# An attention and gated-MLP kernel: values and scores joined, and new slots for attention and operands

## The chip, the cores and the metric

One core of a Trainium2 chip runs the whole program in one launch. The metric is the device time of that core in microseconds. Three runs of the kernel before are given, and one further execution was profiled; all rows come from that execution.

## The reference

Eight batches of eight heads with 576 positions of 64 numbers go through attention in chunks of 64 positions, and the result, 4608 tokens of 512 numbers, through a two-layer MLP with a gate. All is in fp32.

```python
scores = scale * np.matmul(q_c, k_c.transpose(0, 1, 2, 4, 3))   # 64 x 64 per chunk
scores = scores - np.max(scores, axis=-1, keepdims=True)
attn = np.exp(scores)
attn = attn / (np.sum(attn, axis=-1, keepdims=True) + 1e-09)
out = np.matmul(attn, v_c)
...
h = x @ w_in                        # 4608 x 512 by 512 x 2048
g = h * np.clip(h + 3.0, 0.0, 6.0) / 6.0
return g @ w_out                    # 2048 x 512
```

## The kernel before

The tokens are split into nine blocks of 512. An attention (class `Attention`, line 122) handles one block n and one half dp of the heads: `scores` (line 144) makes 64 products of 64x64 into the two banks of one PSUM tile, `soft` (line 161) takes maximum, subtraction, exponential, sum and division in steps 0 to 4, `transpose` (line 187) turns the weights with eight products and a ScalarE copy, and `values` (line 204) makes 64 products of 64x64, which ScalarE copies out. Scores, turned weights and values all use the pool `ps_a`, which holds one such tile. For the blocks n < 3 VectorE then also subtracts the rounded copy from the PSUM tile, to get the low part of the operand (line 234). There are 18 attentions.

A large product is done in three passes of 128x512 fp32r products, high by high, high by low and low by high (`passes`, line 244), so every operand needs a rounded copy (ScalarE) and a remainder (VectorE). 

The work has three parts.

1. **Start** (lines 301 to 381): the two attentions of block 0 in an order written out by hand, with products on dummy data between (`warm_up`), and the first weights turned from 64-bit words into fp32 high and low parts (`convert`, line 99: two ScalarE instructions, shift and addition on VectorE, a ScalarE cast, a VectorE subtraction). Block 0's first product for the first of 16 hidden blocks is written out with it (`part`).
2. **Plain part** (lines 529 to 581): blocks 0 to 2. For each hidden block `ft` there are two slots: an even one with the first product (`mm1`, 12 products into one of the two banks of `ps_h`) and its gate (ReLU on ScalarE, minimum and product on VectorE), and an odd one with the second product of an earlier hidden block (`mm2`, 12 products into four banks of `ps_o`). Other work is put into these slots by number through `plan` (line 476): in each slot the steps of rank under 10 come ahead of the gate (`early_steps`), the others behind it (`late_steps`). During block 0 the weights of `ft + 2` are converted in the slot of `ft`; during blocks 1 and 2 `prepare` (line 401) makes weight combinations and stores them in HBM for the last part.
3. **Steady part** (lines 721 to 746): three superblocks of two blocks, each with a seven-product (Strassen-like) scheme. A superblock has 56 slots of the first product and 56 of the second, each slot six products. In the first product the products come in the order 1, 5, 6, 7, 2, 3, 4 for each of eight hidden pairs p; numbers 2, 3 and 4 go on adding into the banks of 1, 5 and 7, whose sums VectorE must have read by then (`add`, line 597). Number 6 uses `ps_h`, as does number 3 in the second product. Other work hangs at slots through `at` (line 589) and is issued behind the slot's products by rank (`tick`, line 717). `units` (line 654) makes the second product's 28 operand units (ScalarE copy and VectorE subtraction, `split`, line 444), `x_operands` (line 454) the seven operands of the next superblock, and two blocks of attention for the next superblock run meanwhile. GpSimd makes the differences of gated values.

Everything is issued in program order on each engine (`manual_schedule`), and a tile's buffer is taken over when its old readers are done. SyncE issues all transfers in one queue. In the plain part the old attention steps are put by this table and this rank, in which `args` is a list:

```python
later = [(-3, "load_qk"), (2, "scores"), (3, "tiles"), (3, "soft", 0), (3, "soft", 1), (3, "soft", 2), ...
put(at + s, ..., k if name in ("soft", "tiles", "load_qk", "load_v") and args != (2,) else 10 + k)
```

The old steady slots of the four attentions start at 6, 23, 40 and 78 of a superblock, with scores at 0, maximum 1, subtraction 2, sum 8, division 9, turning 12 and values 15 behind; unit k stands at slot 51 + int(1.75 k).

## Time and profile before

| | us |
|---|---|
| median of three runs | 809.33 |
| lowest and highest | 809.21, 809.99 |
| profiled execution | 809.08 |
| its span, first to last instruction | 807.2 |
| PE (TensorE) busy | 796.4 |
| DVE (VectorE) busy | 601.9 |
| ACT (ScalarE) busy | 366.9 |
| POOL (GpSimd) busy | 65.0 |

A busy TensorE is not TensorE at its peak: products overlap, and the end of one is modelled. The pace is read from the starts in the timeline. In a timeline row the columns are start, length, engine, line, operation, output and input tiles, shape and count, and in brackets the idle time of that engine just before, with what ended it. Equal neighbours are merged into one row with a count.

### The profile page before, as it was taken

The page shows a single profiled execution, that of the slowest core. Times are in us where ns is not written, and L with a number is a line of the kernel's source. Part 1 is how long each engine was busy: PE and PEld are TensorE (multiplying, and loading weights), DVE is VectorE, ACT ScalarE, POOL GpSimd, SP SyncE. Part 2 cuts the span into 40 slices and gives each one's busy share as a digit, 9 for nine tenths or more (in the row PEclk, how much of TensorE's full clock was granted, in tenths as well). Part 3 has the DMA queues.
Part 4 walks back from the last instruction along what each step waited for, and adds up shares of the span by engine and source line. Part 5 has one row for each costly group of instructions (what it writes and reads, how often), then busy time and mean ns, then how long its engine had stood idle before and what let it go on. Part 6 is the DMA issues. An engine that isn't in the chain of part 4 may idle for free.

```text
span 807.2 us, 13704 instructions
## 1 busy us (share of the span) xinstructions
PE 796.4 (99%) x5684; PEld 650.0 (81%) x5684; DVE 601.9 (75%) x771; ACT 366.9 (45%) x464; POOL 65.0 (8%) x55
## 2 busy tenths in 40 slices
PE   8999999999999999999999999999999999999997
PEld 5777888888888888888788888888788888888886
DVE  6889867897788682867888776778897856668941
ACT  5878644442453353344473433444634423347330
POOL 0000000000000000222110001222100012221000
PEclk9999999999999999999999999999999999999999
DMA  9980102968888753566556577665566665555463
GB/s 356 410 355 27 53 2 79 310 217 264 291 273 269 246 179 123 203 250 234 179 201 240 207 224 285 252 234 181 201 239 229 214 207 194 205 201 199 176 241 115
DMA packets 50157, 172.85 MB, mean 214 GB/s; under 512 B 4656, under 2 KB 16944, under 8 KB 39472
## 3 DMA queue, kind: packets, MB, share of 16 engines
q1 hardware_dynamic: 50096, 171.99, 60.3%
q8 instruction: 45, 0.74, 0.4%
q14 instruction: 16, 0.13, 0.0%
HBM read 133.17 MB, written 38.80 MB: 213 GB/s over the span
## 4 chain that ended last, share of the span: by engine, by line
PE 86%; DVE 7%; ACT 4%; DMA 1%; issue 1%; SPq 0%; DVEq 0%; ACTq 0%
PE acc L246 19%; PE acc L248 18%; PE acc L247 18%; PE h L246 8%; PE h L248 8%; PE h L247 8%; PE two L216 2%; PE two L154 2%; PE two L198 2%; DMA w<-w_in_out 1%; DVE u L109 1%; DVE u L597 1%; DVE g L609 1%; ACT r L106 1%; ACT u L105 1%
## 5 line engine op out<-in xcount | busy, mean ns | idle before, releaser
L246 PE MATMUL acc<-xop,ws 128*128 128x512 f32 x528 | 208.7, 395 | 0.5
L248 PE MATMUL acc<-xop,ws 128*128 128x512 f32 x528 | 205.7, 390 | 0.0
L247 PE MATMUL acc<-xop,ws 128*128 128x512 f32 x528 | 205.7, 390 | 0.0
L246 PEld LDWEIGHTS acc<-xop,ws 128*128 128x128 f32 x528 | 99.1, 188 | 24.2 <-DVE h L597 2.1
L248 PEld LDWEIGHTS acc<-xop,ws 128*128 128x128 f32 x528 | 99.1, 188 | 20.7
L247 PEld LDWEIGHTS acc<-xop,ws 128*128 128x128 f32 x528 | 99.2, 188 | 19.7
L447 DVE TENSOR_TENSOR xop<-g,xop 128x1024 fp32r<-128x1024 f32 x72 | 87.7, 1238 | 22.5 <-ACT xop L446 22.4
L446 ACT CAST xop<-g 128x1024 fp32r<-128x1024 f32 x72 | 73.2, 1051 | 38.7 <-PE acc L248 21.6
L617 POOL TENSOR_TENSOR g<-g 128x512 f32<-128x512 f32 x24 | 31.0, 1291 | 665.9 <-DVE g L609 665.9
L608 ACT ACTIVATE r<-acc,half 128x512 f32<-128x512 f32 x72 | 49.4, 686 | 71.9 <-DVE acc L597 71.9
L246 PE MATMUL acc<-g,w 128*128 128x512 f32 x192 | 76.3, 397 | 0.0
L246 PE MATMUL h<-x,w 128*128 128x512 f32 x188 | 74.2, 395 | 0.7 <-ACT w L114 0.7
L248 PE MATMUL acc<-g,w 128*128 128x512 f32 x192 | 74.9, 390 | 0.0
L247 PE MATMUL acc<-g,w 128*128 128x512 f32 x192 | 74.8, 390 | 0.0
L248 PE MATMUL h<-x,w 128*128 128x512 f32 x188 | 73.6, 391 | 1.2 <-DVE w L116 1.2
L247 PE MATMUL h<-x,w 128*128 128x512 f32 x188 | 73.2, 390 | 0.0
L609 DVE SCALAR_TENSOR_TENSOR g<-r,acc 128x512 f32<-128x512 f32 x72 | 49.0, 681 | 31.0 <-ACT r L608 31.0
L263 DVE SCALAR_TENSOR_TENSOR r<-r,h 128x512 f32<-128x512 f32 x48 | 32.7, 681 | 32.5 <-ACT r L262 32.5
L246 PE MATMUL h<-xop,ws 128*128 128x512 f32 x144 | 56.2, 391 | 0.0
L247 PE MATMUL h<-xop,ws 128*128 128x512 f32 x144 | 56.0, 389 | 0.0
L248 PE MATMUL h<-xop,ws 128*128 128x512 f32 x144 | 56.0, 389 | 0.0
L262 ACT ACTIVATE r<-h,half 128x512 f32<-128x512 f32 x48 | 32.8, 683 | 47.0 <-PE h L248 47.0
(86 smaller groups left out, 1163.9 us busy)
## 6 DMA issues: line engine op xcount, KB each, us to landing
ws<-b SPq DMA_DIRECT2D x42, 1024.0 KB, 4.8
ws<-a SPq DMA_DIRECT2D x24, 1024.0 KB, 4.9
ws<-a SPq DMA_DIRECT2D x24, 768.0 KB, 4.2
w<-w_in_out SPq DMA_DIRECT2D x16, 1024.0 KB, 18.0
qk<-qk_in SPq DMA_DIRECT2D x16, 1024.0 KB, 6.9
v<-v_in SPq DMA_DIRECT2D x17, 512.0 KB, 5.3
out_t<-o SPq DMA_DIRECT2D x32, 256.0 KB, 3.8
a<-hl SPq DMA_DIRECT2D x32, 256.0 KB, 3.0
```

What stands on the lines that cost most here:

```text
L154: PE.matmul(t[o, a, c if k is None else c % 4, :], lhsT=self.qk[rows, c // 4, 0, c % 4, o], rhs=self.qk[rows, c // 4, 1, c % 4, o], start= ...
L198: PE.transpose(out=self.tp[:, a, i], in_=self.e[:, a, 2 * i:2 * i + 2].rearrange("p c t -> p (c t)"), identity=ident)
L246: PE.matmul(ps, lhsT=a_h, rhs=b_h, start=first, stop=False, skip_group_check=more)
L247: PE.matmul(ps, lhsT=a_h, rhs=b_l, start=False, stop=False, skip_group_check=more)
L248: PE.matmul(ps, lhsT=a_l, rhs=b_h, start=False, stop=last, skip_group_check=more)
L262: ACT.activation(out=r, in_=h, func=AF.Relu, bias=half, scale=1.0 / 6.0)
L263: DVE.scalar_tensor_tensor(out=r, in0=r, scalar=1.0, in1=h, op0=ALU.min, op1=ALU.mult)
L446: ACT.copy(out=t[:, :, 0], in_=src)
L447: DVE.tensor_tensor(out=t[:, :, 1], in0=src, in1=t[:, :, 0].bitcast(F32), op=ALU.subtract)
L608: return (lambda: ACT.activation(out=r, in_=ps, func=AF.Relu, bias=half, scale=1.0 / 6.0), lambda: DVE.scalar_tensor_tensor(out=out, in0=r ...
L609: lambda: DVE.scalar_tensor_tensor(out=out, in0=r, scalar=1.0, in1=ps, op0=ALU.min, op1=ALU.mult))
L617: sub = lambda o, x, y: lambda: POOL.tensor_tensor(out=o, in0=x, in1=y, op=ALU.subtract)
```

## The change

- In the plain part the table PLAIN gives each of eight attentions its own slots (loads, scores, maximum, subtraction, exponential, sum, division, turning, values), and in the steady part STEADY does so for the four attentions of a superblock. Where the values of one attention and the scores of the next have the same slot, `visit` issues the 64 products of the values and the 64 of the scores one behind the other. The values then go to the two banks of `ps_h` (`own_banks`), and each bank is copied out by itself.
- The exponential has rank 10 in the plain part.
- In the steady part a slot may be a fraction: the whole part is the slot, the rest the rank. The unit and operand slots are written out (UNITS, MORE).
- The conversion of weights is a class with a method for each instruction. At the start its instructions for the first three weights, the loads, the first product's passes and the scores of the next block are put in another order; the conversion of the third weight begins at the start.

```diff
+PLAIN = ((0, 0, 0, 9, 10, 10, 12, 13, 16, 18),
+         (4, 14, 20, 21, 21, 22, 24, 24, 29, 30),
+         (31, 34, 36, 37, 37, 37, 38, 38, 42, 43),
+         (36, 44, 43, 45, 46, 47, 48, 48, 53, 55),
+         (52, 56, 55, 56, 56, 57, 58, 59, 64, 65),
+         (60, 65, 65, 66, 66, 66, 67, 67, 69, 71),
+         (67, 73, 71, 72, 72, 72, 73, 74, 78, 79),
+         (71, 80, 79, 80, 80, 80, 81, 81, 85, 86))
+STEADY = ((2.1, 6.6, 7.1, 7.5, 9.0, 12.0, 13.0, 19.1, 20.1),
+          (9.6, 23.3, 20.1, 22.5, 22.5, 30.0, 35.2, 40.6, 41.6),
+          (35.5, 52.0, 41.6, 41.9, 44.5, 47.9, 49.9, 54.6, 71.8),
+          (64.1, 78.6, 71.8, 75.6, 75.7, 78.9, 79.5, 83.6, 87.6))
+UNITS = (-2.9, -1.9, -1.8, 1.8, 3.0, 3.9, 6.4, 11.0, 11.5, 12.0, 12.2, 13.5, 14.1, 14.6, 14.9, 20.9, 23.9, 26.6, 27.5, 28.2, 29.5, 30.7, 32.1, 33.0, 34.6, 34.9, 35.2, 40.1)
+MORE = (43.9, 46.1, 48.2, 53.6, 54.3, 54.6, 56.7)
...
         def multiply(self, heads):
             if heads[0] == 0:
-                self.po = self.psum("o").rearrange("p s (a i t) -> p s a i t", a=2, t=CH)
+                t = self.psum("o")
+                self.apart = isinstance(t, list)
+                self.po = [b.rearrange("p (a i t) -> p a i t", a=2, t=CH) for b in (t if self.apart else [t[:, s] for s in range(2)])]
...
             if self.n >= NSTD:
                 if self.n not in xraw:
                     xraw[self.n] = raw.tile([P, NDP, 2, NT], F32, name="x")
-                ACT.copy(out=as_src(xraw[self.n][:, self.dp]), in_=src)
+                for src, to in parts:
+                    ACT.copy(out=to(xraw[self.n][:, self.dp]), in_=src)
                 return
...
-            ACT.copy(out=as_src(x[:, 0]), in_=src)
-            low.append(lambda: DVE.tensor_tensor(out=as_src(x[:, 1]), in0=src, in1=as_src(x[:, 0]).bitcast(F32), op=ALU.subtract))
+            for src, to in parts:
+                ACT.copy(out=to(x[:, 0]), in_=src)
+                low.append(lambda src=src, to=to: DVE.tensor_tensor(out=to(x[:, 1]), in0=src, in1=to(x[:, 0]).bitcast(F32), op=ALU.subtract))
...
+        load_w(0)
         b0.load_v()
-        load_w(0)
         load_w(1)
         b1.load_v(gp.tile([P, 2, NB // 2, 2 * CH], F32, name="g"))
+        load_w(2)
         a1[0].load_qk()
-        load_w(2)
         load_w(3)
...
+        c0.high()
+        c0.words()
+        b1.soft(0)
+        b1.soft(1)
+        c0.shift()
+        c0.add()
         warm_up(IDLE[3])
+        b1.soft(2)
         b0.turned([0])
         b0.turned([1])
...
+        c0.low()
         finish()
-        next(c1)
+        b1.turned([0])
+        b1.turned([1])
+        c1.shift()
+        c1.add()
+        c2.high()
+        c2.shift()
...
+        for k in (0, 2):
+            part(0, k)
+            part(1, k)
         b1.multiply([0])
         b1.multiply([1])
-        a1[0].scores()
...
+        c1.cast()
         finish()
+        c1.low()
+        c2.words()
+        part(0, 1)
+        part(1, 1)
+        for k in (0, 2, 1):
+            part(2, k)
+            part(3, k)
+            if k == 2:
+                a1[0].scores()
...
+    def own_banks(step):
+
+        return [ps_h.tile([P, NT], F32, name="h") for _ in range(2)] if step == "o" else two_banks(ps_a)
+
+    def visit(a, b):
+
+        a.multiply(range(2))
+        b.scores()
+        a.multiplied(range(2))
+
+    chain = a1 + [Attention(*which) for which in ((2, 0), (2, 1), (3, 0), (4, 0), (4, 1), (3, 1))]
+    for k, (a, slots) in enumerate(zip(chain, PLAIN)):
+        load_qk, load_v, scores, high, sub, exp, total, mult, turn, values = slots
...
+        for step, at in enumerate((high, sub, exp, total, mult)):
+            put(at, lambda step=step, a=a: a.soft(step), 10 if step == 2 else 3 + step)
+        put(turn, a.transpose, 15)
+        if k + 1 < len(PLAIN) and PLAIN[k + 1][2] == values:
+            a.psum = own_banks
+            put(values, lambda a=a, b=chain[k + 1]: visit(a, b), 16)
+        else:
+            put(values, a.values, 16)
...
     def at(slot, *f, rank=0):
 
-        todo.setdefault(slot, []).extend((rank, g) for g in f)
+        todo.setdefault(int(slot // 1), []).extend((slot % 1 + rank, g) for g in f)
...
-        for k in range(4 * 7):
-            at(base + SLOTS - 5 + int(1.75 * k), lambda k=k, unit=unit: unit(k), rank=1)
+        for k, t in enumerate(UNITS):
+            at(base + SLOTS + t, lambda k=k, unit=unit: unit(k))
...
-            for k in range(7):
-                at(base + SLOTS + 44 + 2 * k, more, rank=1)
+            for t in MORE:
+                at(base + SLOTS + t, more)
```

In the steady part `put_steady` puts the four attentions by STEADY in the same way, and a gate that stood in its slot behind nothing (`at(slot + 2, gate)`) now has rank 0.1. In the plain loop the conversion of `ft + 2` issues the same six instructions in the same places, except for `ft = 0`, where only addition, cast and low part are left.

## Rows read from the trace of the kernel before

**Rows 1.** The page: busy us, share of the span and instructions of TensorE.
```profile
PE 796.4 (99%) x5684; PEld 650.0 (81%) x5684; DVE 601.9 (75%) x771; ACT 366.9 (45%) x464; POOL 65.0 (8%) x55
```

**Rows 2.** Timeline of TensorE around one attention's values, late in the plain part.
```profile
283.27 0.39 PE L247 MATMUL h<-x,w 128*128 128x512 f32 x1
283.50 0.39 PE L248 MATMUL h<-x,w 128*128 128x512 f32 x1
283.82 1.16 PE L216 MATMUL two<-e,v 64*64 64x64 f32 x64
284.91 0.50 PE L246 MATMUL acc<-g,w 128*128 128x512 f32 x1
285.25 0.39 PE L247 MATMUL acc<-g,w 128*128 128x512 f32 x1
```

**Rows 3.** Timeline of TensorE at the start: values, then scores.
```profile
21.52 1.16 PE L216 MATMUL two<-g 64*64 64x64 f32 x64
22.50 1.11 PE L154 MATMUL two<-qk 64*64 64x64 f32 x64
```

**Rows 4.** The values' line: products x count, ns min/median/max, first and last start.
```profile
L216 PE MATMUL two<-e,v x1088: 217/218/268, 15.4 to 625.1; 64*64 64x64 f32 x182
```

**Rows 5.** Timeline of ScalarE behind the values of rows 2.
```profile
285.05 1.02 ACT L228 COPY x<-two 128x1024 f32<-128x1024 f32 x1 [0.37 <-PE two L216]
```

**Rows 6.** Groups by shape: half-size copy and half-size subtraction out of PSUM.
```profile
L233 ACT CAST x<-two 128x512 fp32r<-128x512 f32 x4 | 2.1, 585 | 1.0 <-PE two L216 1.0
...
L234 DVE TENSOR_TENSOR x<-two,x 128x512 fp32r<-128x512 f32 x4 | 2.6, 680 | 0.0
```

**Rows 7.** DMA issues on the page: transfers, KB each, median us to landing.
```profile
qk<-qk_in SPq DMA_DIRECT2D x16, 1024.0 KB, 6.9
```

**Rows 8.** Timeline of ScalarE in the plain part.
```profile
56.42 0.67 ACT L262 ACTIVATE r<-h,half 128x512 f32<-128x512 f32 x1
56.99 1.03 ACT L114 CAST w<-u 128x1024 fp32r<-128x1024 f32 x1
```

**Rows 9.** Timeline of TensorE in the plain part.
```profile
59.34 0.50 PE L248 MATMUL h<-x,w 128*128 128x512 f32 x1 [0.53 <-DVE w L116]
```

**Rows 10.** Timeline of VectorE at the start.
```profile
16.79 1.22 DVE L178 TENSOR_REDUCE z<-g 128x16 f32<-128x1024 f32 x1 [0.18 <-ACT g L176]
...
29.54 1.23 DVE L116 TENSOR_TENSOR w<-u,w 128x1024 fp32r<-128x1024 f32 x1 [0.51 <-ACT w L114]
```

**Rows 11.** Timeline of TensorE in the first products of two superblocks.
```profile
395.57 1.03 PE L198 MATMUL two<-ident,e 128*128 128x128 f32 x8
...
397.59 0.39 PE L248 MATMUL acc<-xop,ws 128*128 128x512 f32 x1
398.11 0.50 PE L246 MATMUL acc<-xop,ws 128*128 128x512 f32 x1
...
399.37 0.39 PE L248 MATMUL acc<-xop,ws 128*128 128x512 f32 x1
399.85 0.50 PE L246 MATMUL acc<-xop,ws 128*128 128x512 f32 x1
...
724.99 0.50 PE L246 MATMUL acc<-xop,ws 128*128 128x512 f32 x1
```

**Rows 12.** Timeline of VectorE in the same stretch of the first superblock.
```profile
392.55 1.94 DVE L185 TENSOR_TENSOR e<-e,z 128x1024 f32<-128x1024 f32 x1
...
395.01 1.72 DVE L447 TENSOR_TENSOR xop<-g,xop 128x1024 fp32r<-128x1024 f32 x1
396.65 0.68 DVE L597 TENSOR_TENSOR u<-h,p 128x512 f32<-128x512 f32 x1
397.36 0.69 DVE L597 TENSOR_TENSOR u<-acc,u 128x512 f32<-128x512 f32 x1
...
399.10 0.69 DVE L597 TENSOR_TENSOR h<-acc,u 128x512 f32<-128x512 f32 x1
```

**Rows 13.** Timeline of GpSimd there.
```profile
393.49 2.16 POOL L617 TENSOR_TENSOR t<-g 128x512 f32<-128x512 f32 x1
```

More of the change, by code (lines that the diff above doesn't have):

```diff
@@ L328, in tile_kernel @@
         b0.soft(3, 1)
-        next(c0)
         for a in range(2):
@@ L535, in tile_kernel @@
         over = []
-        c = convert(ft + 2, DVE) if ft + 2 < NFT else None
-        if c:
-            next(c)
-            next(c)
+        c = None
+        if ft + 2 < NFT:
+            c = Convert(ft + 2) if ft else c2
+            if ft:
+                c.high()
+                c.words()
+                c.shift()
+            c.add()
         gt = gate(h)
@@ L545, in tile_kernel @@
         if c:
-            next(c)
-            next(c)
+            c.cast()
+            c.low()
         if len(pending) >= LAG:
@@ L597, in add, with put_steady @@
         return lambda: DVE.tensor_tensor(out=out, in0=x, in1=y, op=ALU.add)
-    def put_steady(n, dp, at_):
-        a = Attention(n, dp)
-        for k, f in ((-6, a.load_qk), (0, a.load_v), (0, a.scores), (1, a.tiles), (1, lambda: a.soft(0)), (2, lambda: a.soft(1)), (2, lambda: a.soft(2)), (8, lambda: a.soft(3)),
-                     (9, lambda: a.soft(4)), (12, a.transpose), (15, a.values)):
-            at(at_ + k, f, rank=2)
+    def put_steady(first, base):
+        four = [Attention(first + k // 2, k % 2, steady_psum) for k in range(2 * NDP)]
+        for k, (a, slots) in enumerate(zip(four, STEADY)):
+            soft = lambda i, a=a: lambda: a.soft(i)
+            load_qk, load_v, scores, high, sub, total, mult, turn, values = (base + t for t in slots)
+            at(load_qk, a.load_qk)
+            at(load_v, a.load_v)
+            if not k or slots[2] != STEADY[k - 1][-1]:
+                at(scores, a.scores)
+            at(high, a.tiles, soft(0))
+            at(sub, soft(1), soft(2))
+            at(total, soft(3))
+            at(mult, soft(4))
+            at(turn, a.transpose)
+            if k + 1 < len(four) and STEADY[k + 1][2] == slots[-1]:
+                a.psum = own_banks
+                at(values, lambda a=a, b=four[k + 1]: visit(a, b))
+            else:
+                at(values, a.values)
     def gated(out, ps):
@@ L641, in first_product @@
                     at(slot + 1, add(acc[6], ps, u4), relu)
-                    at(slot + 2, gate)
+                    at(slot + 2, gate, rank=.1)
                 elif i == 2:
@@ L648, in first_product @@
                     at(slot + 1, add(ps, ps, u2), relu)
-                    at(slot + 2, gate)
+                    at(slot + 2, gate, rank=.1)
                     if i == 3:
-                        at(slot + 2, sub(out, out, gq(0, 0)), sub(t2[p // 2][:, p % 2], gq(1, 1), out))
+                        at(slot + 2, sub(out, out, gq(0, 0)), sub(t2[p // 2][:, p % 2], gq(1, 1), out), rank=.1)
                 tick(slot)
@@ L723, in tile_kernel @@
         if s + 1 < NSUP:
-            for k in range(2 * NDP):
-                put_steady(NSTD + 2 * s + 2 + k // 2, k % 2, base + (6, 23, 40, 78)[k])
+            put_steady(NSTD + 2 * s + 2, base)
         box = {}
```

105 lines of the change are left out of this document (47 added, 58 removed).

## The prediction

> **What bounds the kernel now.** I read the page's busy times first: TensorE works for 99% of the span [rows 1], so the other engines cost something only where TensorE waits for them, and the forecast is a count of what TensorE loses between its 128x512 products. For that I went through TensorE's timeline. A stream of such products starts one every 0.227 us: 283.27 to 283.50 [rows 2]. The same rows show what a small stretch costs. Sixty-four 64x64 products (the values of one attention) stand between the products that start at 283.50 and 284.91, 1.41 us apart, and the product behind them comes another 0.34 later. Beyond the stream's own two steps that is 1.18 + 0.11 = 1.29 us. Every lone values or scores stretch of the plain and steady parts repeats this within 0.06 us; there are 31 of them. The reader should see that the small products themselves don't fill the 1.29: the first of them starts 0.32 behind the last large one.
>
> Once, early in the run, the two kinds stand back to back: values at 21.52, scores at 22.50 [rows 3]. The values took 0.98 there, not 1.29, and nothing lies in the seam. So the change from large to small products and back is paid per stretch, not per set of 64. The view of the values' line adds that the longest of a stretch's products has 268 ns where the median has 218 [rows 4]; the longest are the first after the change, so another 0.05 us is paid once per stretch.
>
> Outside these stretches TensorE stalls at few places: at the start and near 58 and 65 us for the converted weights, and near 398, 400, 565, 567 and 725 us for VectorE's additions.
>
> **The change, part by part.**
>
> *Joined stretches.* The new tables give the values of one attention and the scores of the next the same slot at 43, 55, 65, 71 and 79 of the plain part, and at 20.1, 41.6 and 71.8 in each of the two superblocks that still prepare attention: 5 + 6 = 11 joins. Each saves 1.29 - 0.98 = 0.31, and 0.05 for the first products, so 0.36; 11 x 0.36 = **4.0 us**. The lower bound is nothing (a drain at the seam), the upper 0.4; I take the row of the very pair.
>
> *The two borrowed banks.* The values now fill both banks of the first product's pool, so the next first product waits until one is read out. The ScalarE copy begins 0.07 us after such a stretch ends: 285.05 against 283.82 + 1.16 [rows 2, 5]. It is now two half copies of 0.585, and for n = 2 VectorE's subtraction, also halved, reads the bank again for 0.68 [rows 6]. For n of 3 and more the first bank is free 0.07 + 0.585 = 0.66 us behind the values. The scores cover this: they keep TensorE 0.98 - 0.11 = 0.87 us beyond that end. Cost nothing; without the scores behind them it would be 0.66 less the 0.1 that the change back takes anyway. For n = 2 (slots 43 and 55) it is 0.66 + 0.07 + 0.68 = 1.41 and 0.05 to the product, so TensorE waits 1.46 - 0.87 = 0.59, twice: **-1.2 us**. Before the values, both banks must be free of the preceding hidden block. Its gate is two half-size steps like those of [rows 6], with a wait ahead of each, some 1.4 us behind that block's products; twelve of the second product lie between, 12 x 0.227 = 2.7 us. Nothing. In the steady part the maximum of the slot-41 join waits in VectorE's queue for the scores, with the fourth addition and a gate behind it; the banks that these free are wanted three slots on, 3 x 6 x 0.227 = 4.1 us, and they take about 2. Nothing.
>
> *Loads.* Three of them (q and k at 36 and 71, v at 65) now stand in SyncE's queue in the slot in which the joined or lone stretch still reads the old tile, so they wait there up to one slot; behind them are stores of prepared weights that nobody reads before the steady part. The shortest way from a load to its scores is 52 to 55, four slots of 2.7 us or more with the joined values, against 6.9 to land [rows 7]. Nothing; with the queue blocked for two slots it would still land.
>
> *Exponential behind the gate.* In the old table's helper the test that should send the exponential to the late steps compares a list with a tuple, so the exponential goes early, ahead of the gate's ReLU on ScalarE; the new one has rank 10 and is late. Near 56 us ScalarE did the exponential, the ReLU at 56.42 and, at 56.99, the cast of the weights that TensorE waits for [rows 8]. The ReLU's input was ready before ScalarE idled for the exponential's, so it moves into that idle time, and the cast starts at 56.42, 0.57 earlier; VectorE's gate, which waited for this ReLU, comes earlier too, so the weight's low part keeps pace. TensorE had resumed on that weight's low part at 59.34 [rows 9]; this and everything behind moves by 0.57. The second attention has slack here. Gain **0.6 us**.
>
> *Start.* VectorE sets it. From 16.79, before which it idles 0.18 us for the second exponential, to the third weight's addition it works through the same list, now in another order. The exponential is now ahead of the turned copies on ScalarE, so that idle time goes and the list starts 0.2 earlier. The third weight's cast follows that addition, and its low part, 29.54 to 30.77 [rows 10], releases TensorE. Moving w0 ahead of v and w2 ahead of the next q and k fills SyncE's queue in the order of use, and v is still there before the values want it, as the turned copies come later by one exponential. The scores that adjoined the values in [rows 3] now stand apart, which costs 0.36 in time that TensorE waits anyway. Gain **0.2 us**; bounds 0 (TensorE's own order becomes the limit) and 1.0 (the 0.51 of idle ahead of 29.54 closes as well).
>
> *Units in the steady part.* TensorE's products starting at 398.11 and 399.85 come 0.52 and 0.48 after the one before, and the product behind each 0.11 late again: (0.52 - 0.23 + 0.11) + (0.48 - 0.23 + 0.11) = 0.76 us. The next superblock repeats it, and the last has the second one alone, at 724.99 [rows 11], 0.36. The cause is in VectorE's queue: the multiplication by 1/z (1.94) and the first operand unit's split (1.72) precede the additions that release the accumulating products, at 397.36 and 399.10 [rows 12]. The new table moves that unit from slot 51 to 53 and the second from 52 to 54, behind the first addition's pair, and all else that stood ahead is the same. So the pair's end, 397.36 + 0.69 = 398.05, comes 396.65 - 395.01 = 1.64 earlier, at 396.41, or some 0.3 later than that, as the multiplication now stands right behind a gate that waits for its ReLU. TensorE will want it earlier as well, since neither the stall (0.29) nor the transposes of that place (the 1.03 from 395.57, of which about 0.9 is TensorE's loss) are ahead of it any more: 398.11 - 0.29 - 0.9 = 396.9. The stalls go: 2 x 0.76 + 0.36 = **1.9 us**. What is late next is the unit itself: behind the last addition it needs ReLU, cast and split in a chain, and it would be ready some 0.3 us before the second product wants it.
>
> Here the margin, 0.2 to 0.5 us, hangs on the 1.94 that the multiplication took beside a GpSimd subtraction of 2.16 [rows 13]; the weight's low part, as large, takes 1.23 [rows 10], so 0.7 of collision is in the sum already. The Trainium skill, SBUF — State Buffer, Who interferes with whom, says that a VectorE instruction with two SBUF inputs and a GpSimd one that reads SBUF exclude each other for the whole instruction. By that, the multiplication, which now starts where GpSimd does, could lose the whole subtraction instead of a part, which speaks against this slot: some 0.6 more, a stall of 0.5 us in each of two superblocks, and the sum would be 1.0 less.
>
> **Sum.** 4.0 - 1.2 + 0.6 + 0.2 + 1.9 = 5.5 us. The profiled execution took 809.08 us (span 807.2), 0.25 under the median of the three runs, 809.33; 809.08 - 5.5 = **803.6 us**.
>
> **Rivals.**
> 1. *The additions stay late.* VectorE is the engine behind every stall of the steady part, and the new table bunches units (seven between slots 11.5 and 14.9 of the second product). If the stalls move rather than go, 1.9 is lost: 805.5, and 806.3 if the first units are late by 0.4 in two superblocks. For: the thin margins above. Against: the additions get ranks ahead of the units.
> 2. *More in the first block.* If the start gives its upper bound (0.8 more) and the stalls for weights near 59 and 65 us close too (0.45 each, an estimate: the first had 0.53 of idle [rows 9]), another 1.7: 801.9. For: one VectorE chain feeds them all. Against: that chain keeps its order.
> 3. *The stretches don't join.* If the scores wait for their bank, which the transposed weights leave, or the seam drains, the 4.0 is gone: 807.6. Against: [rows 3] has the seam closed, and the values need that same copy earlier.
> 4. *Slower: the borrowed banks hold TensorE.* The place is the first large product behind each join; the price is the time by which the first half copy ends later than the scores. The gain without the banks' cost is 5.5 + 1.2 = 6.7, so it decides from (6.7 + 1.6) / 11 = 0.75 us a join; at 1.0 it is 809.1 + 11 - 6.7 = 813.4. For: copies stand in ScalarE's queue behind casts, which wait for operand buffers. Against: [rows 5] has ScalarE idle before the copy. The Trainium skill, TensorEngine Tiling (Array Packing), PSUM Bottleneck, says that after such a speedup reading PSUM out may become the limit; [rows 5, 6] bear that out for n = 2 alone.
>
> **How the numbers follow.** Forecast 0.53, rival 1 0.20, rival 2 0.12, rival 3 0.08, rival 4 0.07. The forecast's own range is 802.4 to 804.8: below by the start's other 0.8 and the join's upper bound (11 x 0.04), above by one more collision of 0.7 in each of two superblocks, which past a margin of 0.2 and with a restart of 0.11 is 2 x 0.6. Reaching to rival 2 below and to the end of rival 1 above gives 801.7 to 806.3 with some 0.83. A measurement here tells about 0.2%, 1.6 us, from nothing: under 807.7 is faster. Forecast, rivals 1 and 2 and a part of 3 make 0.88 faster; the rest of 3, 0.05, is no change; rival 4, 0.07, is slower.
>
> **What would show it.** Right: eleven places where 64 values and 64 scores follow without a large product between, 2.34 us from the large product before to the one behind; a TensorE wait of about 0.6 for VectorE's half subtraction behind two of them; no waits for additions near 395, 563 and 720; ReLU ahead of the exponential near 56. Wrong: a large product behind the joins that waits for ScalarE; TensorE idle for an operand split at the start of the second product.

## The result, and the profile after

| | before | after |
|---|---|---|
| median of the runs, us | 809.28 (6 runs) | 802.68 (6 runs, 802.27 to 802.99) |
| ratio, 95% interval | | 0.9916 [0.9903, 0.9929] |
| profiled execution, us | 809.08 | 802.99 |
| its span, us | 807.2 | 801.2 |

The change makes the kernel 6.6 us faster by the medians and 6.0 by the two spans: the profiled execution of before is faster than the median of its kernel, that of after is the slowest of its six. The forecast was 5.5 (803.6), its own range 802.4 to 804.8. The terms below are read from traces, so they have to add up to the 6.0. I go through the trace of after in the order of the prediction's terms.

The page's line of busy times, which answers to [rows 1]:

```profile
PE 791.8 (99%) x5684; PEld 651.3 (81%) x5684; DVE 603.9 (75%) x773; ACT 366.0 (46%) x475; POOL 69.5 (9%) x55
```

TensorE is still the bound, with the same 5684 products. GpSimd's 65.0 became 69.5, which comes back below.

**Joins.** TensorE's timeline at a join in the plain part (compare [rows 2, 3]):

```profile
214.97 0.39 PE L284 MATMUL acc<-g,w 128*128 128x512 f32 x1
215.28 1.16 PE L248 MATMUL h<-e,v 64*64 64x64 f32 x64
216.27 1.11 PE L183 MATMUL two<-qk 64*64 64x64 f32 x64
217.31 0.50 PE L282 MATMUL h<-x,w 128*128 128x512 f32 x1
```

From the large product before to the one behind it are 217.31 - 214.97 = 2.34 us, where two lone stretches took 2 x 1.41. Nine of the eleven joins repeat this.

**Waits.** The view of TensorE's waits from 100 to 780 us of after shows what is left behind the first conversions (total, times, longest):

```profile
PE h L282 <- DVE x L270: 0.9, 2, 0.5
PE acc L282 <- ACT o L328: 0.3, 1, 0.3
```

The first line is the price of the borrowed banks for n = 2. TensorE's timeline at the second of these joins:

```profile
184.07 0.39 PE L284 MATMUL acc<-g,w 128*128 128x512 f32 x1
...
186.94 0.50 PE L282 MATMUL h<-x,w 128*128 128x512 f32 x1 [0.47 <-DVE x L270]
```

and VectorE's at the first, where the two half subtractions stand behind ScalarE's half copies:

```profile
149.86 1.29 DVE L270 TENSOR_TENSOR x<-h,x 128x512 fp32r<-128x512 f32 x2 [0.44 <-ACT x L269]
```

The join is 2.88 long, 0.54 more than the others. The second line of the waits was in no step of the prediction. ScalarE's timeline there:

```profile
221.28 1.06 ACT L205 ACTIVATE e<-e 128x1024 f32<-128x1024 f32 x1 [0.17 <-DVE e L203]
222.25 1.54 ACT L328 COPY o<-acc 128x512 f32<-128x512 f32 x3
227.49 0.59 ACT L328 COPY o<-acc 128x512 f32<-128x512 f32 x1 [3.69 <-DMA out_t<-o]
```

and TensorE's:

```profile
227.42 0.39 PE L284 MATMUL acc<-g,w 128*128 128x512 f32 x1
228.13 0.50 PE L282 MATMUL acc<-g,w 128*128 128x512 f32 x1 [0.32 <-ACT o L328]
```

There are three output tiles, so the fourth output copy of the second block waits until the first output has landed, and TensorE wants that copy's bank at 227.65. It gets it 0.48 late (228.13 - 227.42 is 0.71 instead of 0.23), and the product behind that one pays the slow restart of 0.11: 0.59 in all.

**First block.** TensorE's resumption on the third and on the eighth weight (the latter answers to [rows 9]):

```profile
30.23 0.50 PE L284 MATMUL h<-x,w 128*128 128x512 f32 x1 [0.18 <-DVE w L146]
...
58.20 0.50 PE L284 MATMUL h<-x,w 128*128 128x512 f32 x1 [0.41 <-DVE w L146]
```

The third weight's low part released TensorE at 30.82 before and at 30.23 now: 0.59 earlier. The other resumption moved from 59.34 to 58.20, by 1.14; less 0.59, the exponential's new place is worth 0.55: on ScalarE the cast of [rows 8] now starts at 55.86, right behind the exponential (54.89), and the ReLU lies ahead of both.

In the first block a stall near 65 us is left as it was: the product that waits for the ninth weight starts 0.52 behind the one before it (64.11), in before 0.57.

**Steady part.** The stalls of [rows 11] are gone in all three superblocks. VectorE at the place of [rows 12]:

```profile
391.22 1.22 DVE L214 TENSOR_TENSOR e<-e,z 128x1024 f32<-128x1024 f32 x1
...
392.95 0.68 DVE L661 TENSOR_TENSOR u<-h,p 128x512 f32<-128x512 f32 x1
393.67 0.69 DVE L661 TENSOR_TENSOR u<-acc,u 128x512 f32<-128x512 f32 x1
...
396.92 1.22 DVE L491 TENSOR_TENSOR xop<-g,xop 128x1024 fp32r<-128x1024 f32 x1 [1.75 <-ACT xop L490]
```

GpSimd beside it, which answers to [rows 13]:

```profile
391.38 2.21 POOL L696 TENSOR_TENSOR g<-g 128x512 f32<-128x512 f32 x1 [7.89 <-DVE g L688]
393.67 1.29 POOL L696 TENSOR_TENSOR t<-g 128x512 f32<-128x512 f32 x1
```

and the product of TensorE that reads the second addition:

```profile
394.65 0.39 PE L282 MATMUL acc<-xop,ws 128*128 128x512 f32 x1
```

The first operand unit's split (396.92) now stands behind the additions. The pair ends at 393.67 + 0.69 = 394.36, and the product that reads it starts at 394.65 without a wait: 0.29 of margin.

### The profile page after: what moved, and what is told of

It is laid out like the page before. It is cut to its first block, busy times and chain, and to the rows that moved or that the text cites. A ratio compares the mean times of both kernels' runs of the same rounds, so it can differ in the third digit from the quotient of the medians.

```text
span 801.2 us, 13685 instructions
## 1 busy us (share of the span) xinstructions
PE 791.8 (99%) x5684; PEld 651.3 (81%) x5684; DVE 603.9 (75%) x773; ACT 366.0 (46%) x475; POOL 69.5 (9%) x55
## 4 chain that ended last, share of the span: by engine, by line
PE 89%; DVE 5%; ACT 3%; DMA 1%; issue 1%; DVEq 0%; ACTq 0%
PE acc L282 20%; PE acc L284 19%; PE acc L283 19%; PE h L282 9%; PE h L284 8%; PE h L283 8%; PE two L227 2%; PE two L183 2%; PE h L248 1%; DVE u L137 1%; PE two L248 1%; ACT r L131 1%; ACT w L143 1%; DVE m L201 1%; DMA out_t<-o 1%
## 5 line engine op out<-in xcount | busy, mean ns | idle before, releaser
L491 DVE TENSOR_TENSOR xop<-g,xop 128x1024 fp32r<-128x1024 f32 x72 | 90.2, 1281 | 22.7 <-ACT xop L490 22.7
L696 POOL TENSOR_TENSOR g<-g 128x512 f32<-128x512 f32 x24 | 34.7, 1445 | 657.7 <-DVE g L688 657.7
L687 ACT ACTIVATE r<-acc,half 128x512 f32<-128x512 f32 x72 | 47.4, 686 | 50.6 <-DVE acc L661 50.6
L298 ACT ACTIVATE r<-h,half 128x512 f32<-128x512 f32 x48 | 32.9, 686 | 68.4 <-PE h L284 67.7
L687 ACT ACTIVATE r<-h,half 128x512 f32<-128x512 f32 x24 | 16.5, 689 | 82.9 <-DVE h L661 82.9
```

What stands on the lines that cost most here:

```text
L298: ACT.activation(out=r, in_=h, func=AF.Relu, bias=half, scale=1.0 / 6.0)
L491: DVE.tensor_tensor(out=t[:, :, 1], in0=src, in1=t[:, :, 0].bitcast(F32), op=ALU.subtract)
L687: return (lambda: ACT.activation(out=r, in_=ps, func=AF.Relu, bias=half, scale=1.0 / 6.0), lambda: DVE.scalar_tensor_tensor(out=out, in0=r ...
L696: sub = lambda o, x, y: lambda: POOL.tensor_tensor(out=o, in0=x, in1=y, op=ALU.subtract)
```

## The experiments

Times are medians; a kernel's difference is taken to the kernel before of its own batch (809.28 to 809.32), and through that to after. Each experiment has one profiled execution.

**1. The joins undone, all else kept.** The values go back to slots of their own, ahead of the scores (some of the turnings move with them):

```
-         (31, 34, 36, 37, 37, 37, 38, 38, 42, 43),
+         (31, 34, 36, 37, 37, 37, 38, 38, 41, 42),
...
-          (9.6, 23.3, 20.1, 22.5, 22.5, 30.0, 35.2, 40.6, 41.6),
+          (9.6, 23.3, 20.1, 22.5, 22.5, 30.0, 35.2, 37.6, 39.6),
...
```

> The changed kernel with its eleven joins undone: each of those values stretches one slot (plain part) or one to two slots (steady part) ahead of the scores, in the pool of the scores again; all else as in the changed kernel. Theory (a change between large and small products is paid once per stretch, about 0.39 us by the after-trace: two lone stretches 2 x 1.41 us, a joined one 2.34): 11 x 0.39 = 4.3 us slower, less the two waits of 0.53 us for VectorE's half subtraction that only joined values have, so 3.2 us over the changed kernel, about 806.0; eleven more lone stretches of 1.41 us. Rival (the joins save little, the new slots did it): within 1 us of the changed kernel, under 803.7.

Measured: 805.43 (805.32 to 805.70), ratio 0.9950 [0.9937, 0.9962]; 2.75 above after. The view of TensorE's waits from 100 to 780 us is empty, so the bank waits (2 x 0.54) are gone with the joins, and in this execution the output wait too. How often the runs of after have that wait is not known, so what the joins give is better read against experiment 9 below, which keeps all eleven joins and shows neither wait: 805.43 - 801.24 = 4.2 us, and 803.7 - 799.5 = 4.2 by the spans; 0.38 each.

**2. The seam opened.** One 128x256 product of no use between the values and the scores of each join:

```
+            for _ in range(between):
+                PE.matmul(t[:, 0, :some.shape[-1]], lhsT=some[:, :P], rhs=some, start=True, stop=True)
...
-        b.scores()
+        b.scores(between=1)
```

> The changed kernel with one dummy 128x256 bf16 product of the whole array between the values and the scores of each of the eleven joins, into the bank that the scores then overwrite. One such product alone takes 0.11 us in a stream of its kind. Theory (it is the change of product size that costs): each join gets one change to large and back more, 0.39 + 0.11 = 0.5 us, 11 x 0.5 = 5.5 us slower than the changed kernel at the nine joins that wait for nothing and up to that at the other two, where 0.5 us hides in the wait that is there: 4.4 to 5.5, so 807.1 to 808.2. Rival (the joins gain by fewer waits and issues, not by the product size): 11 x 0.11 = 1.2 us, 803.9.

Measured: 805.57 (805.30 to 805.78), ratio 0.9951 [0.9938, 0.9963]; 2.9 above after. TensorE's timeline of this kernel at the same join:

```profile
214.90 0.39 PE L287 MATMUL acc<-g,w 128*128 128x512 f32 x1
215.22 1.16 PE L251 MATMUL h<-e,v 64*64 64x64 f32 x64
216.32 0.28 PE L177 MATMUL two<-ident 128*128 128x256 bf16 x1
216.53 1.16 PE L186 MATMUL two<-qk 64*64 64x64 f32 x64
217.62 0.50 PE L285 MATMUL h<-x,w 128*128 128x512 f32 x1
```

Large to large it is 217.62 - 214.90 = 2.72, 0.38 more. Twenty such products in a row take 2.36 us at the start of after, 0.11 each; so 0.27 of the 0.38 is the change of kind there and back. That is less than the 0.38 that a join saves, as behind a lone stretch the large product also pays its slow restart. At the two n = 2 joins it adds nothing, as TensorE waits for VectorE there anyway. Nine times 0.38 are 3.4; less the output wait, which this execution does not have, that is 2.8 of the 2.9. Direction as the theory has it, size (4.4 to 5.5) too high by half or more. The product put in differs from the small ones in its shape, its type and its weights (`128x256 bf16` and `128*128` against `64x64 f32` and `64*64`); which of these costs the time is not shown.

**3. The kernel before, with the list and tuple test mended,** so that the exponential goes to the late steps:

```
-            put(at + s, lambda f=getattr(a, name), args=args: f(*args), k if name in ("soft", "tiles", "load_qk", "load_v") and args != (2,) else 10 + k)
+            put(at + s, lambda f=getattr(a, name), args=args: f(*args), k if name in ("soft", "tiles", "load_qk", "load_v") and tuple(args) != (2,) else 10 + k)
```

> The kernel before with one edit: the test on the arguments is repaired, so that the exponential in the plain part has a rank of 10 or more and stands behind the gate. Theory: 0.57 us faster than before, TensorE resumes at 58.8 instead of 59.34 us, and a stall for the weight's cast near 58 us is gone. Rival (the stalls there come from VectorE's queue alone): no change, TensorE resumes at 59.3.

Measured: 808.83 (808.63 to 809.81), ratio 0.9994 [0.9985, 1.0003]. The interval holds no change. In the trace TensorE resumes on the eighth weight at 58.98 instead of 59.34, although this execution's first large product came 0.21 later than before's: 0.57 earlier, the size forecast. The trace carries this term; the times alone don't.

**4. The kernel before with the new slots of the operand units alone,** as whole slots:

```
-        for k in range(4 * 7):
-            at(base + SLOTS - 5 + int(1.75 * k), lambda k=k, unit=unit: unit(k), rank=1)
+        for k, t in enumerate((-3, -2, -2, 1, 3, 3, 6, 11, 11, 12, 12, 13, 14, 14, 14, 20, 23, 26, 27, 28, 29, 30, 32, 33, 34, 34, 35, 40)):
+            at(base + SLOTS + t, lambda k=k, unit=unit: unit(k), rank=1)
```

> The kernel before with the new slots of the 28 units alone (whole slots, old ranks, old attention). Theory (the first unit's split stood ahead of the additions): the waits of TensorE near 398, 400, 565, 567 and 725 us go, 1.9 us faster, about 807.4. Rival (it is the attention's steps at 48 to 52, the sum, the multiplication and the transposes, that make the additions late): only the last superblock's wait goes, 0.4 us, about 808.9.

Measured: 808.17 (808.12 to 808.82), ratio 0.9986 [0.9978, 0.9995]; 1.1 under before. The stalls of the first two superblocks are gone, but the last has two new ones, as TensorE's waits from 300 to 780 us show:

```profile
PE acc L246 <- DVE g L609: 0.4, 1, 0.4
PE acc L247 <- DVE xop L447: 0.2, 1, 0.2
```

VectorE's timeline there has the gate that TensorE waits for (`g<-r,acc`) behind another (`g<-r,h`):

```profile
725.14 0.68 DVE L609 SCALAR_TENSOR_TENSOR g<-r,h 128x512 f32<-128x512 f32 x1
725.74 0.68 DVE L609 SCALAR_TENSOR_TENSOR g<-r,acc 128x512 f32<-128x512 f32 x1
```

**5. The same, and three gates of each hidden pair behind the slot's steps of rank 0** (among them another gate), but ahead of the units:

```
-                    at(slot + 2, gate)
+                    at(slot + 2, gate, rank=.5)
...
```

> The kernel before with the new slots of the units alone, and the three gates that the change puts behind a slot's other steps put there too. With the slots alone the gain was 1.1 where 1.9 was expected: the stalls of the first two superblocks were gone, and the last had two new waits of 0.41 and 0.21 with VectorE's gates ahead. Theory (the gates' place matters where units and gates share a slot): the two waits are gone as well, time 807.4 (807.0 to 807.9). Rival (the whole numbers in place of fractions for the units' slots, or the attention's steps, make the waits): they stay, 808.2.

Measured: 806.86 (806.80 to 807.51), ratio 0.9968 [0.9956, 0.9981]; 2.5 under before by the medians. In the traces TensorE's last large product starts 2.10 earlier (800.39 against 802.49), in an execution that resumed on the third weight 0.16 later than before's (30.98 against 30.82); so the steady part itself gains some 2.3. Both waits are gone, and VectorE has the two gates in the other order:

```profile
724.25 0.68 DVE L609 SCALAR_TENSOR_TENSOR g<-r,acc 128x512 f32<-128x512 f32 x1
724.85 0.68 DVE L609 SCALAR_TENSOR_TENSOR g<-r,h 128x512 f32<-128x512 f32 x1
```

So, with these whole slots, the steady part's gain takes both edits, the units' slots and the ranks of the gates. After without the gates' ranks was not run.

**6. After with the old order of the first loads.**

```
-        load_w(0)
         b0.load_v()
+        load_w(0)
         load_w(1)
         b1.load_v(gp.tile([P, 2, NB // 2, 2 * CH], F32, name="g"))
-        load_w(2)
         a1[0].load_qk()
+        load_w(2)
```

> The changed kernel with the old order of the first loads (v ahead of w0, the next q and k ahead of w2). Theory (VectorE's list sets the start, the loads only have to be there): within 0.3 us of the changed kernel, and TensorE's wait for the third weight's low part near 30 us stays 0.35 to 0.5. Rival (the earlier w0 lets the first conversion move ahead): 0.5 us or more slower, ScalarE waits for w0 until 12.6 us instead of about 11.4.

Measured: 803.41 (802.99 to 803.78), ratio 0.9925 [0.9913, 0.9938]; 0.73 above after by the medians, while the ranges touch at 802.99. ScalarE of this kernel:

```profile
22.73 1.14 ACT L123 ACTIVATE u<-w 128x1024 f32<-128x1024 f32 x1 [0.70 <-DMA w<-w_in_out]
```

and TensorE:

```profile
24.40 1.45 PE L403 MATMUL h<-x,w 128*128 128x512 f32 x4 [0.84 <-ACT x L269]
```

The third weight lands too late; ScalarE waits for it with the values' copy (23.77) queued behind, and TensorE waits for that copy. It resumes on the third weight's low part at 30.82, as in before.

**7. After with the old order of the first block's instructions, the new loads kept.** The diff is that of the start, reversed:

```
+        c0.high()
+        c0.words()
         for a in range(2):
             b0.soft(4, a=slice(a, a + 1))
             b0.turn([a])
-        c0.high()
-        c0.words()
-        b1.soft(0)
-        b1.soft(1)
...
```

> The changed kernel with the old order of the instructions at the start (the new order of the loads stays; the third weight is converted in the loop again). Theory (the new order gives what TensorE's resume point near 30 us shows, 30.82 before and 30.23 after): 0.6 us slower than the changed kernel, 803.3, with two waits of TensorE for the third weight instead of one. Rival (that difference is the scatter of the first transfers, 0.2 to 0.4 us from run to run): within 0.3 us of it.

Measured: 802.54 (802.14 to 803.06), ratio 0.9915 [0.9901, 0.9928]; the same as after. TensorE resumes on the third weight at 30.12. The rival, that the 0.59 is scatter, does not hold over all the traces: the nine kernels with the new order of the loads resume there between 29.92 and 30.50, the five with the old order (before and experiments 3 to 6) between 30.82 and 31.65. So the start's 0.6 comes from the loads alone, and the new order of instructions adds nothing that can be seen.

**8. The n = 2 joins ahead of the last quarter of a second product,** so that three large products cover the half subtractions:

```
+            if et == NET - 2 and inside:
+                inside()
...
+            if a.n < NSTD:
+                inner[values] = lambda a=a, b=chain[k + 1]: visit(a, b)
+            else:
+                put(values, lambda a=a, b=chain[k + 1]: visit(a, b), 16)
...
```

> The changed kernel with the two joins of n = 2 (slots 43 and 55) put between the third and the last quarter of the second product's twelve products instead of behind them, so that three products of 0.227 us follow the scores before a bank of the first product's pool is wanted. Theory (TensorE waits there for VectorE's half subtraction, 0.53 us, and 0.68 us of products cover it): the two waits go, 1.07 us faster than the changed kernel, 801.6. Rival (the values then wait for the gate of the hidden block just done, some 1.5 us behind its products, against 2.0 us of second product): a wait of VectorE or ScalarE ahead of the values, no gain.

Measured: 802.04 (801.80 to 802.57), ratio 0.9907 [0.9892, 0.9922]; 0.64 under after. The first wait is gone; the second shows 0.24 idle. VectorE there:

```profile
184.12 1.80 DVE L462 TENSOR_TENSOR a<-a 128x256 f32<-128x256 f32 x4
185.84 1.28 DVE L270 TENSOR_TENSOR x<-h,x 128x512 fp32r<-128x512 f32 x2
```

and TensorE:

```profile
186.58 0.50 PE L282 MATMUL h<-x,w 128*128 128x512 f32 x1 [0.24 <-DVE x L270]
```

By the starts this place gains nothing yet: the product comes 0.64 behind the one before it instead of 0.23, and the next pays a slow restart once more, some 0.5 in all against the 0.54 of after.

**9. The same, with the half subtractions ahead of those four sums** (`L462` above):

```
                 inside()
+                finish()
```

> The changed kernel with both stretches of the block with two-bank values put ahead of the last quarter of a second product, as before, and VectorE's two low halves of the values put right behind them, ahead of the prepared sums that share the slot. Theory (the 0.24 us that the second of these stretches still left was VectorE doing four sums first): no wait of TensorE at either, both stretches leave the large products 2.34 apart; time 801.7 (801.3 to 802.2), 0.9 to 1.0 under the changed kernel. Rival (what is late is ScalarE's copy of the values, not the order of VectorE): the wait stays at 0.2 or more, 802.0.

Measured: 801.24 (801.13 to 801.45), ratio 0.9897 [0.9884, 0.9911]. All eleven joins are 2.34 long. All of its runs lie under the lowest of after's (802.27); it is the fastest kernel of this study, 1.4 us under after by the medians. The two bank waits are 1.07 of it; the output wait is not in its profile either.

**10. After with the exponential of the sixth attention behind the output copies,** since it had kept the first of them back, and its row sum and multiplication a slot later with it:

```
-         (60, 65, 65, 66, 66, 66, 67, 67, 69, 71),
+         (60, 65, 65, 66, 66, 67, 68, 68, 69, 71),
```

> The changed kernel with one attention's exponential at slot 67 instead of 66 and its sum and multiplication at 68 instead of 67, so that ScalarE copies block 1's output banks ahead of that exponential. Theory (the stall of 0.48 and 0.11 us near 228 us comes from the exponential of 1.07 us ahead of the first output copy, which makes the transfer that frees the fourth output tile land late): the stall goes, 0.6 us faster than the changed kernel, 802.1. Rival (it is the transfer's own time of 4 to 5 us in a busy queue, whatever the copy's place): the fourth copy still waits for the landing and TensorE for it, no change.

Measured: 809.85 (808.78 to 810.89), ratio 1.0004 [0.9995, 1.0013]: the whole gain is lost. ScalarE:

```profile
226.22 0.59 ACT L328 COPY o<-acc 128x512 f32<-128x512 f32 x1 [3.54 <-DMA out_t<-o]
226.70 1.06 ACT L205 ACTIVATE e<-e 128x1024 f32<-128x1024 f32 x1
```

and TensorE, the transposes and two of the products behind them:

```profile
232.97 1.94 PE L227 MATMUL two<-ident,e 128*128 128x128 f32 x8 [4.80 <-DVE e L214]
...
236.41 0.63 PE L283 MATMUL h<-x,w 128*128 128x512 f32 x1
236.84 0.63 PE L284 MATMUL h<-x,w 128*128 128x512 f32 x1
```

The exponential now stands behind the fourth copy, which waits for the landing. It ends at 227.76, but the row sum starts 2.09 later, as in its new slot it stands behind a gate's step whose input ScalarE makes later still. VectorE:

```profile
229.24 0.69 DVE L304 TENSOR_TENSOR g<-r,g 128x512 fp32r<-128x512 f32 x1 [4.69 <-ACT g L302]
229.85 1.21 DVE L207 TENSOR_REDUCE z<-e 128x16 f32<-128x1024 f32 x1
```

The multiplication and the transposes follow late, and TensorE idles 4.80 us. Moving work behind an instruction that waits for a transfer moved it behind the transfer. That alone need not cost anything: in the kernel before, the same exponential stood behind the fourth copy too,

```profile
227.31 1.07 ACT L176 ACTIVATE e<-e 128x1024 f32<-128x1024 f32 x1
```

and TensorE did not wait, since its transposes were due only at 234.97. The new table has them at 228.93.

**11. Experiment 9, with that exponential between the third and the fourth copy.**

```
+            if et == NET - 1 and n == 1:
+                ahead_of_last.pop()()
...
```

> The same, and the exponential that shares a slot with the four output copies of the second block put between the third and the fourth of them. Theory (the wait near 227.4 is the fourth copy waiting for the landing of the first, which the exponential had delayed by 1.1): the first copy starts 1.0 to 1.3 earlier and the fourth ends before TensorE wants its bank; the wait of 0.3 to 0.5 is gone in all executions, the fastest runs change least, the median falls by 0.3 to 0.6 against the kernel beside it: 801.2 (800.9 to 801.6). Rival (the exponential's chain is as short of time): the transposes near 229 wait, and the time is that of the kernel beside it or above.

Measured: 801.55 (800.81 to 802.03), ratio 0.9899 [0.9883, 0.9914]; no gain over experiment 9, whose profile had no output wait to begin with; here TensorE comes 0.16 late at that place. The first copy did start earlier, at 220.25 (221.21 there), but the fourth, which needs its landing, began at 226.38 (225.90 there). SyncE's queue issued the first output only at 221.67, when it was through with seven transfers of prepared weights. So here the landing was set not by ScalarE's copy, but by what stands ahead of the output in the queue.

**12. After with one load, the sixth attention's v, two slots later.** In the kernel before it came behind the outputs, in after ahead of them:

```
-         (60, 65, 65, 66, 66, 66, 67, 67, 69, 71),
+         (60, 67, 65, 66, 66, 66, 67, 67, 69, 71),
```

> The changed kernel with one load moved: the sixth attention's v (512 KB) two slots later, so that SP issues it behind the four output transfers of the second block, as the kernel before did, and not ahead of them. Putting the exponential behind three of the output copies had let the first start 0.96 earlier and yet its transfer was issued only when SP was through with seven transfers ahead of it, and landed no earlier. Theory (the landing that the fourth copy waits for is set by what is queued ahead of it, the v load among it): at some 400 GB/s the 512 KB are 1.3 us; the first output lands 0.9 to 1.3 earlier, near 226.4, the fourth copy ends before 227.4 and TensorE's wait there is gone; 802.3 (802.0 to 802.6) with fewer runs near 803. Rival (the landing is set by the issue of the output alone): it lands 4.6 behind its issue as before, the wait stays in the profile and the time is 802.7.

Measured: 802.17 (801.79 to 802.48), ratio 0.9908 [0.9892, 0.9925]; 0.5 under after. SyncE's queue in after (start, duration, what is issued):

```profile
216.53 0.35 SPq L171 DMA_DIRECT2D v<-v_in  x1
216.98 2.34 SPq L469 DMA_DIRECT2D b<-hl  x4
219.36 2.42 SPq L473 DMA_DIRECT2D b<-w  x3
222.84 5.59 SPq L329 DMA_DIRECT2D out_t<-o  x4
```

and in this kernel:

```profile
223.00 3.57 SPq L329 DMA_DIRECT2D out_t<-o  x4
...
227.09 0.44 SPq L171 DMA_DIRECT2D v<-v_in  x1
```

and ScalarE's fourth output copy in this kernel:

```profile
225.62 0.59 ACT L328 COPY o<-acc 128x512 f32<-128x512 f32 x1 [1.67 <-DMA out_t<-o]
```

The first output is issued at nearly the same time, but the fourth copy that needs its landing starts at 225.62 instead of 227.49, and TensorE's wait is gone. The median time to land of the four outputs is 2.6 against 4.6 us.

The other traces bear this out for the landing. Where the load stands as in after, right ahead of the prepared weights (after and experiments 2 and 6 to 11), the fourth copy starts 3.7 to 4.7 us behind the issue of the first output; here it is 2.6, and in experiment 1, where the load is issued 3 us earlier (213.45), 2.5. But only after, experiment 8 and, by 0.16, experiment 11 have TensorE wait, so the wait itself hangs on some tenths. And the times do not show a gain clear of noise: the runs here and those of after (802.27 to 802.99) overlap.

Nor is the load the only thing that changed. In the kernel before, with the load behind the outputs, the fourth copy also came 3.98 behind the issue (226.83 against 222.85), and TensorE wanted its bank only near 228.85. In after TensorE is there 1.2 us earlier, while the first output is issued no earlier (222.84), as the exponential now stands ahead of the first copy. Taking the load away is enough to end the wait in this trace; which part each of the two has in it is not separated.

## Why the prediction came out right

| term | forecast, us | measured, us | from |
|---|---|---|---|
| eleven joins | +4.0 | +4.2 | experiments 1 and 9 |
| banks, two joins of n = 2 | -1.2 | -1.07 | 2 x 0.54 in the trace of after |
| exponential behind the gate | +0.6 | +0.55 | resumption on the eighth weight; experiment 3 |
| start | +0.2 | +0.59 | resumption on the third weight |
| units in the steady part | +1.9 | +2.3 | traces of experiment 5 and of before |
| output wait | none | -0.59 | trace of after |
| sum | 5.5 | 6.0 | 6.0 by the spans of before and after |

That the sum lies within 0.5 is in part luck. The start, the units, the joins and the banks gave some 1.1 more than was put down for them, the start for a reason that the prediction had put at nothing, and the output wait, which was in no term, took 0.6 back.

**The joins** are what was forecast, to 0.02 each. Large to large, a join saves 2 x 1.41 - 2.34 = 0.48, but it spans one of the stream's own steps less (0.23), so 0.25 is the small products' part; the rest, 0.13 of the 0.38, is the slow restart. The forecast had 0.36: the same 0.25, and 0.11 of restart, the one late product behind the change. Behind each change the next few products too come up to 10 ns further apart, some 0.02 in all. Rival 3 (the stretches don't join) has no place left: nine joins are 2.34 long in the trace of after, and experiment 2 opened the seam and paid for it.

**The borrowed banks** came out as worked out: nothing for n of 3 and more, a wait of 0.47 idle for n = 2 at both joins, with VectorE's half subtraction as the releaser. Experiments 8 and 9 show that this price was one of place: a quarter of a second product covers it, if VectorE does the half subtractions first. Rival 4 did not happen; ScalarE was free when the copy was wanted.

**The exponential** is right in size and cause, by the trace of experiment 3.

**The start** is right in sign and wrong in cause. The prediction said that VectorE sets it, gave the gain to the exponential's place ahead of the turned copies, and costed the order of the loads at nothing. Experiments 6 and 7 show the reverse: with the old loads the gain is gone and TensorE resumes at 30.82 as before, with the old order of instructions it stays. What failed is the sentence that w0 and w2 ahead merely fill SyncE's queue in the order of use. In before, ScalarE's first step on the first weight had waited 2.96 us for it to land; that step began at 12.66, and in after at 11.39. Of rival 2 this is a part: the start gave 0.4 of its other 0.8, but the stalls near 58 us (0.41 idle) and 65 us stayed.

**The units** went as forecast: the additions of [rows 12] come ahead of the split, the pair ended 0.29 before the product wanted it (0.2 to 0.5 was forecast), and rival 1 did not happen. Of the 0.4 above the forecast a half shows in the trace: before has four smaller delays that were not counted (products 0.27 to 0.34 behind the one before, from 366.06, 533.54, 723.32 and 727.16, 0.29 in all), and experiment 5 has one of 0.09. The prediction passed over the gates' small ranks as if they belonged to no term; experiments 4 and 5 show that 1.3 of the 2.5 hang on them there.

The collision did not come as feared, and for a reason that the rows show. The multiplication started 0.16 ahead of GpSimd's subtraction and took its undisturbed 1.22; GpSimd took 2.21 where its next one took 1.29, so it lost 0.92 of the 1.06 in which both ran. In before it was the other way round. The prediction laid the multiplication's 1.94 to the subtraction of [rows 13], but that one began 0.94 behind it. Another had begun 0.43 ahead of it, and lost nothing:

```profile
392.12 1.29 POOL L617 TENSOR_TENSOR g<-g 128x512 f32<-128x512 f32 x1 [8.29 <-DVE g L609]
```

The Trainium skill, SBUF — State Buffer, Who interferes with whom, has it that the order of issue decides which of the two blocks; the trace agrees, with those numbers. The prediction had taken from that section that the two exclude each other, and not that the first one loses nothing.

**The output wait** is the term that was missing. The prediction followed the moved loads to their own users (four slots against 6.9 us), and of what stands behind them in the queue it named the stores of prepared weights alone. Yet the v load went from behind the second block's four outputs to ahead of them. Nor did it ask what the exponential, now ahead of the first output copy, holds back. Whether the wait is part of why the runs of after spread over 0.7 us is not shown: those of before, whose profile has no such wait, spread over 0.8.

## What to carry to other kernels

On an engine that is busy 99% of the time, count changes between kinds of products, not the products: two small stretches set back to back cost 0.38 us less here than two that stand alone, and a resource borrowed for it (here two banks) is free wherever other products stand between the loan and its next use. When a load is moved, look not only at who waits for it but at what it now precedes in its queue, above all at transfers whose landing frees a buffer. Work behind an instruction that waits for a transfer comes behind the transfer too: it may stand there only if TensorE wants it late enough, as in before (transposes at 234.97) and not in experiment 10.

## What was not expected of the hardware

Experiment 10 lost more than its idle time. Its stretches (columns as on the page: PE, PEld, DVE, ACT, POOL, then the granted clock, DMA share and GB/s):

```profile
230.00:231.00 1.00, 0.00 (x0) 0.00 (x0) 1.00 (x1) 0.00 (x0) 0.00 (x0) 0.78 0.83 319
231.00:233.00 2.00, 0.03 (x1) 0.06 (x1) 1.90 (x5) 0.00 (x0) 0.00 (x0) 0.50 0.26 107
233.00:235.00 2.00, 2.00 (x9) 2.00 (x10) 1.97 (x3) 0.05 (x1) 0.00 (x0) 0.50 0.00 0
...
237.00:238.00 1.00, 1.00 (x5) 0.79 (x4) 0.20 (x1) 0.00 (x0) 0.00 (x0) 0.81 1.09 332
```

During the 4.80 us of idle the granted clock fell to 0.50, the 1.2 GHz level, and it came back to 2.4 GHz only some 4 us after TensorE was at work again. In between the transposes took 1.94 where eight of them take 1.03 elsewhere, and six large products came about 0.43 apart instead of 0.23. That is 0.9 + 6 x 0.2 = 2.1 us on top of the 4.8. Together they are 6.9; less the 0.59 of output wait that after has at this place and this kernel has not, 6.3, against the 6.2 us between the two profiles' spans (807.4 and 801.2). The medians lie 7.2 apart.

The other one is how far an output's landing moves with what was issued ahead of it: with the issue at 222.84 and 223.00, the fourth copy got its tile at 227.49 and 225.62. The view by stretches of after has the DMA engines' share at 1.05 to 1.08 from 220 to 226 us; without the load ahead of the outputs (experiment 12) it falls to 0.58 from 222 to 224. So in after the 512 KB of the v load were not hidden beside the outputs, but delayed them.
